# Attention and a routed mixture of experts on one core: logits of the last four tiles, stores of x, and the first passes of the second product in another order

## The chip, the cores and the metric

The kernel runs on 1 core of one Trainium2 chip. The metric is device time in microseconds (us). PE is the matrix engine, PEld its weight loads, DVE the vector engine, ACT the scalar engine, POOL the general engine (it also starts the indirect transfers), and SP the engine whose queue starts the plain transfers and the transposing ones.

## The reference

```python
def _attn_ref(q, k, v):                 # (4, 8, 768, 64)
    k_sum = k.reshape(B, H, nb, block, D).max(axis=3)      # blocks of 32
    v_sum = v.reshape(B, H, nb, block, D).mean(axis=3)
    scores_l = scale * q @ k^T, only where |i - j| < 16
    scores_s = scale * q . k_sum + log(block)
    a = softmax over [scores_l, scores_s]
    return a @ concat([v, v_sum])

def _moe_ref(x, w_gate, w_noise, noise, w1, w2):           # x is (3072, 512)
    noisy = x @ w_gate + log1p(exp(x @ w_noise)) * noise
    top2 = the two largest of 8; weights = softmax over the two
    for e in range(8):
        for k in range(2):
            mask = top2[:, k] == e
            h = maximum(x[mask] @ w1[e], 0)                # 512 -> 1024
            out[mask] += weight * (h @ w2[e])              # 1024 -> 512
```

The output of attention, heads side by side, is the x of the experts.

## The kernel before, in words

**Stages.** The 3072 tokens are 24 tiles of 128 (six for each of four batches). A loop over `t` (from -2 to 22) runs attention as a software pipeline: iteration `t` computes scores of tile `t + 2`, transposes the probabilities of tile `t + 1`, multiplies tile `t` by v (`av`, L323), and finishes tile `t - 1`: `norm` (DVE, L332 to L338) writes X in float32, `x_pe` (PE, L360) and `x_copy` (ACT, L366) make its transpose, `norm_hi` (ACT, L345, or DVE by `norm_hi_dve`, L349, for the iterations in `DVE_HI`) rounds it to float16, `norm_lo` (POOL, L352) writes what the rounding lost, and `x_out` (SP, L355) stores both halves to `xd` in DRAM. X has two buffers, the rounded pair `xr` has three, so `norm_hi` of tile t waits until the store of tile t - 3 has landed, and X of tile t until both readers of tile t - 2 are done.

**Routing.** Tiles are routed in batches of four. `gate_gt` (PE, L378) makes the logits, transposed; `gate_gc` (DVE, L385), `gate_gl` (PE, L389) and `gate_gd` (DVE, L394) turn them round; `gate_a` (ACT, L406 and L408), `gate_b`, `gate_m` (DVE, L416 to L438) pick the two best; `gate_p` (ACT, L445) makes a weight; `gate_c` (PE, L452 to L456) and `gate_d`, `gate_e` (DVE, L470 to L498) give every token its place in its expert's list; `gate_v`, `gate_o`, `gate_f` (DVE, L504 to L535) build one-hot matrices, `gate_t` (PE, L545) multiplies them, and `gate_u` (DVE, L549) adds the result to ACC, which `decode` (DVE, L556 to L562) turns into the table of token ids and weights. Batch b has tiles 4b to 4b + 3. Expert 0's first three chunks of 128 rows come only from tiles 0 to 11, so they are decoded early (`TB0`); the rest needs all six batches (`finish_table`).

**Experts.** A list holds up to 816 rows, in seven chunks. `x_gather` (POOL, L86) fetches a chunk of rows into one of four buffers `xg`, and `x_trans` (SP, L668) transposes it into `xte`. `mm1` is the first product: for each of eight slices f of the hidden width 12 matmuls (high weights by high x, low weights by high x, high weights by low x), over rows 0 to 383 (`half` 0) or 384 to 815 (`half` 1), followed by ACT's high half of h (`hth`, L691) and DVE's low half (`htl`, L692). `mm2` is the second product: for a chunk, `mm2_high` makes two passes of 8 matmuls with the high weights (by `hth`, then `htl`), `mm2_low` one with the low weights, then DVE scales (L748) and POOL scatters the result into the output. The output is first cleared by `clear` (SP, L778), eight transfers of 768 KB that read zeros from buffer 3 of `xg`.

**What sets the order.** Everything is issued in program order on each engine and each queue. In the loop, `at(time, function, ...)` puts a step behind a numbered point of an iteration (time 21.9 is near the end of iteration 21). After the loop the order is written out by hand: the end of attention, the routing of batches 3 to 5 and the first product of expert 0 (half 0) are interleaved. `og` is a PSUM tile of two banks that carries ranks (`gate_c`), table products (`gate_t`) and the product of slice 0.

Of the kernel before, what the change touches and what calls it, by code (L numbers as in the profile page):

```python
# [8 lines left out]
F32 = mybir.dt.float32  # L9
# [11 lines left out]
P = 128  # L21
# [3 lines left out]
DM = H * D  # L25
# [34 lines left out]
def attn_moe(ctx, tc, qt, kt, vt, wgn, noise, w1, w2, out):  # L60
# [289 lines left out]

    def norm_lo(t):
        nc.gpsimd.tensor_tensor(XR[t][:, DM:], X[t], XR[t][:, 0:DM], op=OP.subtract)  # L352

# [319 lines left out]

    def mm1_pe(e, half, f, ph=None):
        c0, c1 = (0, H0) if half == 0 else (H0, CAP)
        n = c1 - c0
        ph = PH[f] = bank()[:, 0] if ph is None else ph
        w = WT[e]
        x = XTE[e]
        k = 0  # L680
        for wn, xo in (("w1h", 0), ("w1l", 0), ("w1h", DC)):
            for c in range(DC):
                nc.tensor.matmul(ph[:, :n], w[wn][:, c, f * P:(f + 1) * P], x[:, xo + c, c0:c1],  # L683
                                 start=(k == 0), stop=(k == 11))
                k += 1

    def mm1_out(e, half, f):
# [45 lines left out]

    def mm2_high(e, c, hook=None):
        PY[c] = psum.tile([P, 512], F32, name="pt", bufs=2)
        mm2_pass(e, c, "w2h", HT[0], 0, PY[c])
        if hook:
            hook()
        mm2_pass(e, c, "w2h", HT[1], 1, PY[c])
# [30 lines left out]
    def at(t, f, *a):  # L770
        todo.setdefault(round(t, 3), []).append((f, a))
# [27 lines left out]
    w_alloc(0)  # L799
    W0 = [4, 6, 10, 14]  # L800
    for i in range(4):
# [7 lines left out]
    KL = [-3, -3, -3, -1, -1, -1]  # L809
    VL = [(1, 2), (7, 8), (12, 13)]  # L810
    for b in range(B - 1):
# [49 lines left out]
    for c in range(3):  # L861
        at((20.2, 20.8, 21.2)[c], x_gather, 0, c, P * BATCH[GROUP0][0])
        at((20.9, 21.2, 21.8)[c], x_trans, 0, c)

    DVE_HI = (4, 5, 8, 10, 16, 18)

# [67 lines left out]
    x_out(NT - 3)  # L934
    for i in range(4):
        clear(XG[3].bitcast(F32), 3)

# [13 lines left out]
    og = psum.tile([P, 2, 512], F32, name="o")  # L951
    gate_c(4, og)
    mm1_pe(0, 0, 0, og[:, 1])
    x_pe(NT - 2)
    x_copy(NT - 2)
    x_pe(NT - 1)
    x_copy(NT - 1)
    gate_p(4)
    for t in range(NT - 2, NT):
        norm_hi(t)  # L960
        norm_lo(t)
        x_out(t)
    for i in range(4):
        clear(XG[3].bitcast(F32), 3)
    for x in HT:
        nc.gpsimd.memset(x[:, :, CAP:], 0.0)
    gate_d(4, og)
    gate_e(4)
    gate_f(3)
    gate_gt(5)  # L970
    gate_gc(5)
    gate_gl(5)
    mm1_out(0, 0, 0)
    gate_t(3, og)
    gate_gd(5)
    gate_a(5)
    mm1_pe(0, 0, 1)
    gate_v(4)
    gate_u(3, og)
    gate_o(4)  # L980
    gate_b(5)
    gate_m(5)
    gate_p(5)
    w_hi(0, 4)
    gate_f(4)
    mm1_out(0, 0, 1)
    mm1_pe(0, 0, 2)
    gate_c(5, og)
    gate_d(5, og)
    gate_e(5)  # L990
    w_hi(0, 5)
    mm1_pe(0, 0, 3)
    gate_t(4, og)
    mm1_out(0, 0, 2)
    gate_u(4, og)
    gate_v(5)
    mm1_out(0, 0, 3)
    w_hi(0, 6)
    mm1_pe(0, 0, 4)
    gate_o(5)  # L1000
    mm1_out(0, 0, 4)
    w_hi(0, 7)
    mm1_pe(0, 0, 5)
    gate_f(5)
    mm1_out(0, 0, 5)
    for f in range(6, FC):
        mm1(0, 0, f)

    def finish_table():
        gate_t(5, og)  # L1010
        gate_u(5, og)
        decode(TB.rearrange("p e c w -> p (e c) w"), 0, NS)
# [6 lines left out]

    mm2_high(0, 0, finish_table)  # L1020
    mm2_high(0, 1)
    assert not todo, todo
    for x in PREV:
        nc.gpsimd.memset(x, 0.0)
    count_over(og)
    for c in range(2):
        mm2_low(0, c, None)
    mm2(0, 2, None)
    k = 0
# [139 lines left out]
```

## Time and profile before

| what | us |
|---|---|
| median of 3 runs | 714.16 (712.05, 714.16, 715.68) |
| profiled execution | 712.75 |
| its span, first to last instruction | 711.0 |
| PE busy, of the span | 669.7 |
| DVE / POOL / ACT busy | 318.1 / 253.3 / 233.9 |
| start of expert 0's second half of rows (first L683 with 432 columns) | 193.90 |

In the span the granted clock of PE is 0.984 of full speed in the mean. Attention fills the first 147 us, expert 0's first half of rows and the table the time to 194 us, and all the other products the rest. In rows of the timeline, the numbers are start and duration in us, and the brackets give the idle time before and what ended it.

### The profile page before, as it was taken

The page shows a single profiled execution, that of the slowest core. Times are in us where ns is not written, and L with a number is a line of the kernel's source. Part 1 is how long each engine was busy: PE and PEld are TensorE (multiplying, and loading weights), DVE is VectorE, ACT ScalarE, POOL GpSimd, SP SyncE. Part 2 cuts the span into 40 slices and gives each one's busy share as a digit, 9 for nine tenths or more (in the row PEclk, how much of TensorE's full clock was granted, in tenths as well). Part 3 has the DMA queues.
Part 4 walks back from the last instruction along what each step waited for, and adds up shares of the span by engine and source line. Part 5 has one row for each costly group of instructions (what it writes and reads, how often), then busy time and mean ns, then how long its engine had stood idle before and what let it go on. Part 6 is the DMA issues. An engine that isn't in the chain of part 4 may idle for free.

```text
span 711.0 us, 13980 instructions
## 1 busy us (share of the span) xinstructions
PE 669.7 (94%) x5552; PEld 386.2 (54%) x5552; DVE 318.1 (45%) x663; ACT 233.9 (33%) x534; POOL 253.3 (36%) x437
## 2 busy tenths in 40 slices
PE   7998879759999999999999999999999999999993
PEld 6776667536455554555455446545654555455442
DVE  5658888868542452345125413521451154222210
ACT  2978888724040450143014202410350043002100
POOL 3444445420523605632444143323424341440141
PEclk9999999989999999999999999999999999999997
DMA  9999897594682984498339525931792198210020
GB/s 288 302 253 353 260 337 240 164 341 174 164 208 64 286 218 117 145 272 256 102 82 259 182 89 132 287 125 65 177 294 82 63 212 194 90 62 27 20 86 35
DMA packets 101767, 126.26 MB, mean 178 GB/s; under 512 B 60457, under 2 KB 65329, under 8 KB 101692
## 3 DMA queue, kind: packets, MB, share of 16 engines
q1 hardware_dynamic: 89548, 89.00, 45.0%
q0 software_dynamic: 12144, 36.28, 16.7%
q8 instruction: 46, 0.75, 0.5%
q14 instruction: 29, 0.24, 0.1%
HBM read 87.57 MB, written 26.21 MB: 160 GB/s over the span
## 4 chain that ended last, share of the span: by engine, by line
PE 78%; DMA 10%; DVE 5%; ACT 2%; SPq 1%; issue 1%; POOL 1%; POOLq 0%; DVEq 0%
PE h L683 36%; PE pt L731 33%; PE pt L728 3%; DMA q<-in_qt_dram 2%; DMA stg<-in_w_dram 2%; DMA htl<-in_vt_dram 2%; DMA xg<-xd,tb 1%; DMA vw<-in_vt_dram 1%; PE s L290 1%; PE pt L310 1%; DMA xte<-xg 1%; DMA kb<-in_kt_dram 1%; DVE nm L297 1%; ACT p L304 1%; PE pt L235 1%
## 5 line engine op out<-in xcount | busy, mean ns | idle before, releaser
L683 PE MATMUL h<-xte,w1h 128*128 128x384 f16 (+1 forms) x1016 | 198.8, 337 | 0.3 <-DVE htl L692 0.2
L691 ACT ACTIVATE hth<-h 128x384 f16<-128x384 f32 (+1 forms) x127 | 64.1, 508 | 328.7 <-PE h L683 328.5
L86 POOL DMA_INDIRECT out_dram<-y,tb x48 | 56.1, 1169 | 256.2 <-DVE y L750 224.3
L683 PEld LDWEIGHTS <-w1h 128*128 128x128 f16 x1024 | 99.9, 98 | 80.1 <-issue 3.4
L731 PEld LDWEIGHTS <-hth 128*128 128x128 f16 x768 | 75.0, 98 | 91.1 <-issue 1.6
L692 DVE SCALAR_TENSOR_TENSOR htl<-h,hth 128x384 f16<-128x384 f32 (+1 forms) x127 | 73.1, 581 | 100.2 <-ACT hth L691 99.7
L683 PE MATMUL h<-xte,w1l 128*128 128x384 f16 (+1 forms) x508 | 109.0, 338 | 0.0
L750 DVE SCALAR_TENSOR_TENSOR y<-pt,tb,prev 128x512 f32<-128x512 f32 x42 | 31.5, 751 | 172.4 <-PE pt L731 168.0
L731 PE MATMUL pt<-w2l,hth 128*128 128x512 f16 x384 | 90.8, 379 | 0.5 <-DVE w2l L629 0.5
L731 PE MATMUL pt<-w2h,hth 128*128 128x512 f16 x384 | 90.7, 379 | 0.2 <-DVE y L748 0.2
L731 PE MATMUL pt<-w2h,htl 128*128 128x512 f16 x384 | 90.7, 379 | 0.0
L86 POOL DMA_INDIRECT xg<-xd,tb x56 | 61.0, 1090 | 79.8 <-DMA xte<-xg 46.6
L683 PEld LDWEIGHTS <-w1l 128*128 128x128 f16 x512 | 50.5, 99 | 39.0 <-issue 1.2
L731 PEld LDWEIGHTS <-htl 128*128 128x128 f16 x384 | 37.5, 98 | 45.1
L352 POOL TENSOR_TENSOR xr<-x,xr 128x512 f16<-128x512 f32 x24 | 28.1, 1172 | 75.7 <-ACT xr L345 50.6
L304 ACT ACTIVATE p<-s,nm 128x118 f32<-128x118 f32 x192 | 50.5, 375 | 0.8
L612 ACT ACTIVATE w2h<-stg 128x1024 f16<-128x1024 f32 x32 | 33.5, 1051 | 43.2 <-DMA stg<-in_w_dram 43.2
L629 DVE SCALAR_TENSOR_TENSOR w2l<-stg,w2h 128x1024 f16<-128x1024 f32 x32 | 38.8, 1222 | 19.6 <-ACT w2h L612 19.6
L86 POOL DMA_INDIRECT prev<-out_dram,tb x42 | 43.0, 1024 | 10.8 <-issue 10.5
L629 DVE SCALAR_TENSOR_TENSOR w1l<-stg,w1h 128x1024 f16<-128x1024 f32 x28 | 34.3, 1225 | 16.5 <-ACT w1h L612 16.5
L290 PE MATMUL s<-kx,q 64*64 64x118 f32 x768 | 26.1, 272 | 7.8 <-DMA q<-in_qt_dram 4.4
L310 PE MATMUL pt<-ident,p 128*118 128x128 f32 x192 | 29.8, 293 | 3.9 <-ACT xt L366 3.4
(162 smaller groups left out, 572.6 us busy)
## 6 DMA issues: line engine op xcount, KB each, us to landing
stg<-in_w_dram SPq DMA_DIRECT2D x64, 512.0 KB
hth<-in_vt_dram SPq DMA_DIRECT2D x8, 780.0 KB
vw<-in_vt_dram SPq DMA_DIRECT2D x32, 195.0 KB
q<-in_qt_dram SPq DMA_DIRECT2D x24, 256.0 KB
xd<-xr SPq DMA_DIRECT2D x24, 256.0 KB
out_dram<-xg SPq DMA_DIRECT2D x8, 768.0 KB
kb<-in_kt_dram SPq DMA_DIRECT2D x6, 768.0 KB
htl<-in_vt_dram SPq DMA_DIRECT2D x16, 195.0 KB
```

Source lines behind the costliest of these rows:

```text
L86: return nc.gpsimd.indirect_dma_start(**kw)
L290: nc.tensor.matmul(s[64 * blk:64 * blk + 64, a, hp, :], q[d, hp, blk], k[d, hp, blk, :], start=False, stop=hp == HP - 1, skip_group_check= ...
L304: nc.scalar.activation(PE_[t][:, a, hp, :], SC[t][:, a, hp, :], AF.Exp, bias=NM[t][:, 1, a, hp:hp + 1], scale=0.125)
L310: nc.tensor.transpose(pt[:NK, hp, :], PE_[t][:, a, hp, :], ident)
L352: nc.gpsimd.tensor_tensor(XR[t][:, DM:], X[t], XR[t][:, 0:DM], op=OP.subtract)
L612: nc.scalar.activation(WT[e][n + "h"][:, i % 4, :], SG[e, i], AF.Copy, scale=sc)
L629: nc.vector.scalar_tensor_tensor(lo, SG[e, i], sc, hi, op0=OP.mult, op1=OP.subtract)
L683: nc.tensor.matmul(ph[:, :n], w[wn][:, c, f * P:(f + 1) * P], x[:, xo + c, c0:c1], start=(k == 0), stop=(k == 11))
L691: nc.scalar.activation(hh[:, f, c0:c1], ph, AF.Relu)
L692: nc.vector.scalar_tensor_tensor(hl[:, f, c0:c1], ph, 0.0, hh[:, f, c0:c1], op0=OP.max, op1=OP.subtract)
L731: nc.tensor.matmul(py, hx[:, f, c * P:c * P + P], w[:, f, :], start=first, stop=final, skip_group_check=True)
L750: nc.vector.scalar_tensor_tensor(y, py[:, :d], gw, pv[:, :d], op0=OP.mult, op1=OP.add)
```

## The change

In the loop: the three gathers of expert 0 (`x_gather`, chunks 0 to 2) are issued together at 20.2, and their transposes move from 20.9, 21.2 and 21.8 to 21.02, 22.02 and 22.02, behind `v_load` and stores of x. The iterations 16 and 18 leave `DVE_HI`. The load of the last quarter of expert 0's w1 moves from iteration 14 to 12 (its splitting from 17.9 to 19.9 down to 15.9 to 17.9), the loads of batch 3's v from iterations 12 and 13 to 13 and 14.

Behind the loop: `norm_lo` of the last two tiles moves to DVE; the logits of batch 5 (`gate_gt`, `gate_gc`) come before the first product of slice 0, and `gate_gl` between its first four and last eight matmuls; the table steps of batches 3 and 4 come after `gate_b` and `gate_m` of batch 5; all eight clears come behind the store of tile 23; `finish_table` stands in front of the second product; there, the high passes of chunks 0, 1 and 2 come first (chunk 2 in a bank of the first product), then their low passes.

```diff
-    def norm_lo(t):
-        nc.gpsimd.tensor_tensor(XR[t][:, DM:], X[t], XR[t][:, 0:DM], op=OP.subtract)
+    def norm_lo(t, engine=nc.gpsimd):
+        engine.tensor_tensor(XR[t][:, DM:], X[t], XR[t][:, 0:DM], op=OP.subtract)
...
-    def mm1_pe(e, half, f, ph=None):
+    def mm1_pe(e, half, f, ph=None, hook=None):
...
                 k += 1
+            if hook and k == DC:
+                hook()
...
-    def mm2_high(e, c, hook=None):
-        PY[c] = psum.tile([P, 512], F32, name="pt", bufs=2)
+    def mm2_high(e, c, hook=None, py=None):
+        PY[c] = psum.tile([P, 512], F32, name="pt", bufs=2) if py is None else py
...
-    W0 = [4, 6, 10, 14]
+    W0 = [4, 6, 10, 12]
...
-    VL = [(1, 2), (7, 8), (12, 13)]
+    VL = [(1, 2), (7, 8), (13, 14)]
...
-        at((20.2, 20.8, 21.2)[c], x_gather, 0, c, P * BATCH[GROUP0][0])
-        at((20.9, 21.2, 21.8)[c], x_trans, 0, c)
-
-    DVE_HI = (4, 5, 8, 10, 16, 18)
+        at(20.2, x_gather, 0, c, P * BATCH[GROUP0][0])
+        at((21.02, 22.02, 22.02)[c], x_trans, 0, c)
+
+    DVE_HI = (4, 5, 8, 10)
...
-    for i in range(4):
-        clear(XG[3].bitcast(F32), 3)
...
-    gate_c(4, og)
-    mm1_pe(0, 0, 0, og[:, 1])
+    gate_p(4)
     x_pe(NT - 2)
     x_copy(NT - 2)
+    gate_c(4, og)
     x_pe(NT - 1)
     x_copy(NT - 1)
-    gate_p(4)
-    for t in range(NT - 2, NT):
-        norm_hi(t)
-        norm_lo(t)
-        x_out(t)
-    for i in range(4):
+    gate_d(4, og)
+    gate_e(4)
+    gate_gt(5)
+    gate_gc(5)
+    norm_hi(NT - 2)
+    norm_lo(NT - 2, nc.vector)
+    x_out(NT - 2)
+    mm1_pe(0, 0, 0, og[:, 1], lambda: gate_gl(5))
+    gate_gd(5)
+    gate_a(5)
+    norm_hi(NT - 1)
+    norm_lo(NT - 1, nc.vector)
+    x_out(NT - 1)
+    for i in range(8):
         clear(XG[3].bitcast(F32), 3)
     for x in HT:
         nc.gpsimd.memset(x[:, :, CAP:], 0.0)
-    gate_d(4, og)
-    gate_e(4)
-    gate_f(3)
-    gate_gt(5)
-    gate_gc(5)
-    gate_gl(5)
-    mm1_out(0, 0, 0)
-    gate_t(3, og)
-    gate_gd(5)
-    gate_a(5)
-    mm1_pe(0, 0, 1)
-    gate_v(4)
-    gate_u(3, og)
-    gate_o(4)
     gate_b(5)
     gate_m(5)
     gate_p(5)
+    mm1_out(0, 0, 0)
+    mm1_pe(0, 0, 1)
+    gate_c(5, og)
+    gate_f(3)
+    mm1_pe(0, 0, 2)
     w_hi(0, 4)
...
+    gate_t(3, og)
+    mm1_out(0, 0, 1)
+    gate_v(4)
+    gate_o(4)
+    mm1_pe(0, 0, 3)
+    gate_u(3, og)
+    gate_f(4)
     w_hi(0, 5)
...
+    mm1_out(0, 0, 2)
+    gate_v(5)
+    mm1_pe(0, 0, 4)
     gate_t(4, og)
+    gate_o(5)
...
     def finish_table():
-        gate_t(5, og)
-        gate_u(5, og)
...
-    mm2_high(0, 0, finish_table)
+    finish_table()
+    mm2_high(0, 0)
     mm2_high(0, 1)
+    mm2_high(0, 2, None, bank()[:, 0])
...
-    for c in range(2):
+    for c in range(3):
         mm2_low(0, c, None)
-    mm2(0, 2, None)
```

The order of instructions at three places. PE, behind the last attention output: rows of the difference from the end of `gate_c(4)` (L456) to the first matmul of slice 0 (L683); `x` is X, `xt` its copied transpose, `wg` the gate weights.

```order
 L456 LDWEIGHTS ones
 L456 MATMUL o<-m,ones 128x8
+L360 MATMUL pt<-ident,x 128x128 x4
+L378 MATMUL pt<-xt,wg_144 32x128 x16
 L683 LDWEIGHTS w1h_298
 L683 MATMUL o<-xte,w1h_298 128x384
```

The transposes of tile 23 and the logits now stand between the ranks and slice 0. The same difference behind slice 0's last matmul, where they stood:

```order
 L683 LDWEIGHTS w1h_298
 L683 MATMUL o<-xte,w1h_298 128x384
-L360 MATMUL pt<-ident,x 128x128 x8
-L378 MATMUL pt<-xt,wg_144 32x128 x16
-L389 MATMUL pt<-ident,lt 128x128
```

All of it has moved in front; L389 (`gate_gl`) is now behind slice 0's fourth matmul.

DVE, from the end of `gate_e(4)` (L498), before; `lt` and `lg` are the logits on their way round, `rh`, `lh`, `oc` the one-hot matrices, `htl` the low half of slice 0:

```order
L498 SCALAR_TENSOR_TENSOR rf<-qf,pf 128x8
L535 TENSOR_TENSOR rh<-oc,val 128x672 x2
L385 COPY lt<-pt 128x128
L692 SCALAR_TENSOR_TENSOR htl<-o,hth 128x384
L394 COPY lg<-pt 128x64
L512 TENSOR_TENSOR wa<-wa,p_2901 128x4
```

and now:

```order
L498 SCALAR_TENSOR_TENSOR rf<-qf,pf 128x8
L385 COPY lt<-pt 128x128
L352 TENSOR_TENSOR xr<-x,xr 128x512
L394 COPY lg<-pt 128x64
L352 TENSOR_TENSOR xr<-x,xr 128x512
L416 TENSOR_TENSOR nz<-sp,noi 128x32
```

The table steps and slice 0's low half went behind; the two low halves of x came in, around `lg`.

SP, from the load of w2's last quarter (L607), before; `xd<-xr` is a store of x, `xte<-xg` a transpose of gathered rows, `htl<-in_vt_dram` a v load, `out_dram<-xg_160` a clear:

```order
L607 DMA stg<-in_w_dram 128x2x512
L668 DMA_TRANSPOSE xte<-xg_157 128x8x128
L257 DMA htl<-in_vt_dram 96x520 x2
L355 DMA xd<-xr 128x1024
L668 DMA_TRANSPOSE xte<-xg_158 128x8x128
L668 DMA_TRANSPOSE xte<-xg_159 128x8x128
L355 DMA xd<-xr 128x1024 x3
L778 DMA out_dram<-xg_160 128x3x512 x4
L355 DMA xd<-xr 128x1024 x2
```

and now:

```order
L607 DMA stg<-in_w_dram 128x2x512
L257 DMA htl<-in_vt_dram 96x520 x2
L355 DMA xd<-xr 128x1024
L668 DMA_TRANSPOSE xte<-xg_157 128x8x128
L355 DMA xd<-xr 128x1024
L668 DMA_TRANSPOSE xte<-xg_158 128x8x128
L668 DMA_TRANSPOSE xte<-xg_159 128x8x128
L355 DMA xd<-xr 128x1024 x4
L780 DMA out_dram<-xg_160 128x3x512 x8
```

The last v load and the store of tile 18 passed the first transpose, the store of tile 19 the second; the clears went behind the last store (L780 is the line of `clear` in the changed kernel).

More of the change, by code (lines that the diff above doesn't have):

```diff
@@ L683, in mm1_pe @@
                 nc.tensor.matmul(ph[:, :n], w[wn][:, c, f * P:(f + 1) * P], x[:, xo + c, c0:c1],
-                                 start=(k == 0), stop=(k == 11))
+                                 start=(k == 0), stop=(k == 11), skip_group_check=hook is not None)
                 k += 1
+            if hook and k == DC:
+                hook()
     def mm1_out(e, half, f):
@@ L983, in attn_moe @@
     gate_p(5)
+    mm1_out(0, 0, 0)
[3 more added lines that the diff above has]
+    mm1_pe(0, 0, 2)
     w_hi(0, 4)
[L985 to L988, printed above, removed]
     gate_d(5, og)
     gate_e(5)
+    gate_t(3, og)
[5 more added lines that the diff above has]
+    gate_f(4)
     w_hi(0, 5)
-    mm1_pe(0, 0, 3)
+    mm1_out(0, 0, 2)
+    gate_v(5)
+    mm1_pe(0, 0, 4)
     gate_t(4, og)
-    mm1_out(0, 0, 2)
+    gate_o(5)
+    mm1_out(0, 0, 3)
     gate_u(4, og)
-    gate_v(5)
-    mm1_out(0, 0, 3)
     w_hi(0, 6)
[L999 to L1002, printed above, removed]
     mm1_pe(0, 0, 5)
     gate_f(5)
+    mm1_out(0, 0, 4)
+    mm1_pe(0, 0, 6)
     mm1_out(0, 0, 5)
-    for f in range(6, FC):
-        mm1(0, 0, f)
+    w_hi(0, 7)
+    mm1_pe(0, 0, 7)
+    gate_t(5, og)
+    mm1_out(0, 0, 6)
+    gate_u(5, og)
+    mm1_out(0, 0, 7)
     def finish_table():
-        gate_t(5, og)
-        gate_u(5, og)
         decode(TB.rearrange("p e c w -> p (e c) w"), 0, NS)
```

## The prediction, made before the result

> **What bounds the kernel now.** I read the page first, then busy time in stretches around the hand-over from attention to the experts, then the waits in 142 to 165 us, and last the engines' own timelines there. The stretches (us; busy time of PE, PEld, DVE, ACT, POOL with counts; granted clock; DMA share; GB/s):
>
> ```profile
> 146.73:149.11 2.38, 0.00 (x1) 0.03 (x2) 0.39 (x3) 0.63 (x1) 1.09 (x1) 1.00 1.09 295
> 149.11:152.52 3.41, 3.41 (x12) 1.73 (x13) 1.83 (x3) 0.00 (x0) 0.06 (x1) 0.56 0.93 353
> 152.52:159.22 6.70, 2.73 (x42) 1.95 (x40) 4.99 (x14) 2.59 (x6) 2.57 (x5) 0.97 1.05 407
> 159.22:163.20 3.98, 3.85 (x17) 2.38 (x18) 3.24 (x11) 0.46 (x2) 0.00 (x0) 0.57 1.05 406
> 163.20:176.28 13.08, 13.08 (x90) 8.14 (x89) 11.36 (x44) 6.71 (x11) 0.00 (x0) 1.00 0.36 136
> 193.90:711.00 517.10, 505.45 (x2904) 266.15 (x2903) 173.07 (x230) 114.55 (x176) 177.91 (x303) 0.99 0.54 146
> ```
>
> From 193.90, where the second half of expert 0's first product starts, PE is busy to the end; nothing the change touches lies there, so those 517.1 us stay and only the start of that half can move. The loss is between 146.73 and 163.20: PE idles for 2.38 us, runs 3.41 us at a clock of 0.56, is busy for 2.73 of 6.70 us, and then runs at 0.57 again. What ends those waits (waiter, releaser, total us, times, longest):
>
> ```profile
> PE pt L389 <- DVE lt L385: 3.6, 1, 3.6
> PE o L683 <- DMA xte<-xg: 2.4, 1, 2.4
> DVE pos L470 <- PE o L683: 1.7, 1, 1.7
> ACT xr L345 <- DMA xd<-xr: 3.8, 1, 3.8
> ```
>
> So PE first waits for transposed rows; then it computes product 0, while DVE's ranks of tiles 16 to 19 wait for that product in the same tile; then DVE is late with the copy of the last logits. ACT's 3.8 us goes on to POOL and from POOL to DVE, as the next rows show: the x of tile 23 starts at 149.20, after 2.05 us of waiting.
>
> **The table's chain, step by step.** After the change DVE runs nearly without a break, so I lay its steps out from 145.65, where it starts to normalise tile 22. All times in this part are on the clock of the trace before. Prices are distances between starts in these rows (start, busy us, engine, line, operation):
>
> ```profile
> 143.69 0.18 DVE L416 TENSOR_TENSOR nz<-sp,noi 128x32 f32<-128x32 f32 x1
> 145.65 0.16 DVE L332 TENSOR_SCALAR r<-s 128x8 f32<-128x8 f32 x1
> 146.76 0.15 DVE L332 TENSOR_SCALAR r<-s 128x8 f32<-128x8 f32 x1
> 149.20 0.69 DVE L338 TENSOR_TENSOR x<-s,ri 128x512 f32<-128x512 f32 x1 [2.05 <-POOL xr L352]
> 155.14 2.26 POOL L352 TENSOR_TENSOR xr<-x,xr 128x512 f16<-128x512 f32 x2 [5.97 <-ACT xr L345]
> 156.35 1.07 DVE L498 SCALAR_TENSOR_TENSOR rf<-qf,pf 128x8 f16<-128x8 f16 x1
> 166.91 0.18 DVE L470 TENSOR_TENSOR pos<-o,bs 128x32 f32<-128x32 f32 x1
> 168.33 0.55 DVE L692 SCALAR_TENSOR_TENSOR htl<-h,hth 128x384 f16<-128x384 f32 x1
> 169.03 0.16 DVE L512 TENSOR_TENSOR wa<-wa,p 128x4 f32<-128x4 f32 x1
> 170.12 0.55 DVE L692 SCALAR_TENSOR_TENSOR htl<-h,hth 128x384 f16<-128x384 f32 x1
> 170.59 0.68 DVE L504 TENSOR_TENSOR lh<-iotar,rf 128x512 f16<-128x512 f16 x1
> 171.72 0.55 DVE L692 SCALAR_TENSOR_TENSOR htl<-h,hth 128x384 f16<-128x384 f32 x1
> 172.19 1.62 DVE L535 TENSOR_TENSOR rh<-oc,val 128x672 f16<-128x672 f16 x2
> 173.72 0.55 DVE L692 SCALAR_TENSOR_TENSOR htl<-h,hth 128x384 f16<-128x384 f32 x1
> 178.79 0.33 DVE L549 TENSOR_TENSOR acc<-acc,o 128x168 f32<-128x168 f32 x1 [1.23 <-PE o L545]
> 180.47 1.02 POOL L86 DMA_INDIRECT xg<-xd,tb  x1 [22.76 <-DVE oc L561]
> ```
>
> That gives: one norm 1.11 (145.65 to 146.76); gate_b with gate_m 1.96 (143.69 to 145.65); gate_d with gate_e 1.42 (166.91 to 168.33); gate_v 1.09; one low half of h 0.47 (170.12 to 170.59); gate_o 1.13; gate_f 1.53; gate_u 0.3; from the last gate_u to the first gather of the remaining rows 1.68 (178.79 to 180.47). PE's, ACT's and the clears' prices:
>
> ```profile
> 137.64 1.08 PE L378 MATMUL pt<-xt,wg 128*32 128x128 f32 x32 [0.35 <-ACT pts L313]
> 167.90 0.74 PE L545 MATMUL o<-rh,lh 128*128 128x168 f16 x8
> 171.08 0.81 PE L683 MATMUL h<-xte,w1l 128*128 128x384 f16 x4
> 173.03 0.81 PE L683 MATMUL h<-xte,w1l 128*128 128x384 f16 x4
> 188.45 1.89 PE L731 MATMUL pt<-w2h,hth 128*128 128x512 f16 x8 [0.20 <-DVE y L748]
> 190.17 1.89 PE L731 MATMUL pt<-w2h,htl 128*128 128x512 f16 x8
> 193.90 0.89 PE L683 MATMUL h<-xte,w1h 128*128 128x432 f16 x4
> 154.43 1.15 ACT L345 ACTIVATE xr<-x 128x512 f16<-128x512 f32 x2
> 159.90 0.23 ACT L406 ACTIVATE e<-lg 128x32 f32<-128x32 f32 x1 [3.94 <-DVE wa L512]
> 160.16 0.23 ACT L408 ACTIVATE sp<-e 128x32 f32<-128x32 f32 x1
> out_dram<-xg SPq DMA_DIRECT2D x8, 768.0 KB
> ```
>
> One product of 12 matmuls takes 1.95 (171.08 to 173.03), a pass of 8 in the second product 1.72, gate_t about 0.6.
>
> *Transposed rows.* PE now asks for them only after the logits, at about 150.3. The three gathers stand one behind another on POOL, right after the table of the first ids, and no cast or low half of POOL stands between them. The last transpose landed at 149.1 before (146.73 plus 2.38), with one store of x less in front of it, but with the second and third gather behind a low half on POOL. Even without any gain there the wait of 2.4 is covered by the logits; if it came back, each us later than 150.3 would cost one.
>
> *Stores of x.* The store of tile 18 goes ahead of the first transpose, so ACT's cast of tile 21 and POOL's low half no longer wait. X of tile 23 then needs no buffer that is held: two norms end at 145.65 + 2.22 = 147.87. Next late is DVE itself.
>
> *Logits first.* gate_o(3) to 149.0, gate_d(4) and gate_e(4) to 150.4: they no longer wait 1.7 for product 0, and no POOL work runs beside them, which in the rows at 155.14 and 156.35 goes with an operation on 8 elements taking 1.07. On PE the transposes of tile 23 start at 147.9; with their four matmuls (0.6), ACT's copy (0.65) and gate_gt (1.08) the logits are there at 150.3. The copy lt ends at 150.6, norm_lo of tile 22 on DVE at 151.3. That operation is new on DVE: I take 0.69, the row of x at 149.20, of the same size; POOL's 1.13 (half of 2.26) is the upper bound, and the low half of h, of the same kind on three quarters of the size, at 0.55 the lower one. PE runs four matmuls of product 0 (0.65) and turns the logits round by 151.25, and lg is copied by 151.45.
>
> *A new wait.* The diff puts norm_lo(23) on DVE behind norm_hi(23), which stands on ACT behind gate_a(5). From lg that is 0.49 (159.90 to the end of sp), 0.58 for the cast and some 0.15 of hops, so DVE idles to 152.7. Behind it queue gate_b(5) and all later steps: norm_lo to 153.4, gate_b and gate_m to 155.3, product 0's low half (ACT's part ends at 155.6) to 156.1, gate_f(3) 157.6, gate_d and gate_e(5) 159.05, low half 1 159.5, gate_v(4) 160.6, gate_o(4) 161.75, gate_u 162.05, gate_f(4) 163.55.
>
> *PE behind it.* Product 0 ends at 152.55, product 1 at 154.5; gate_c(5) waits for gate_m to 155.4; product 2 ends at 157.45, gate_t(3) at 158.2, products 3 and 4 at 162.1. There PE waits 1.5 for gate_f(4), and gate_t(4) ends at 164.2. Products 5 to 7 (5.85) end at 170.05, and gate_t(5) at 170.6; DVE's last gate_f is done at 163.55 + 0.47 + 2.22 + 0.47 + 0.3 + 1.53 = 168.55, in time.
>
> *Table and second product.* The last gate_u starts at 170.75, and one low half (0.47) now stands between it and the decoding, so the gathers start at 170.75 + 0.47 + 1.68 = 172.9 against 180.47. From there to the second half's first matmul before took 193.90 - 180.47 = 13.43 (four gathers, four transposes), which gives 186.3. PE's own way is 9 passes of 1.72 = 15.5 from 170.6, to 186.1: high passes of three chunks first leave DVE 10.3 us for the low weights, so that wait is gone, but the end is set by the rows. The half starts at 186.3 instead of 193.90: 7.6 us gained.
>
> *Attention's last tiles.* Two casts go from DVE to ACT, and the last quarter of expert 0's first weights is loaded and split two tiles earlier, the last v loads one tile later.
>
> ```profile
> 108.47 0.43 DVE L349 CAST xr<-x 128x512 f16<-128x512 f32 x1 [0.92 <-DMA xd<-xr]
> L622 DVE SCALAR_TENSOR_TENSOR w1l<-stg,w1h 128x512 f16<-128x512 f32 x3 | 2.1, 685 | 0.0
> 105.28 1.04 PE L290 MATMUL s<-kx,q 64*64 64x118 f32 x32 [1.75 <-DMA q<-in_qt_dram]
> ```
>
> For DVE this is at most 2 x 0.43 + 0.92 + 2 x 0.69 = 3.2 less; on the other side ACT gets two casts of 0.58, and 512 KB instead of the 390 of half a batch of v go ahead of a q for which PE waits already: 122 KB at 353 to 407 GB/s are 0.3. Between +3.2 and -1.5 I take +0.5, nearer to the lower end, because what DVE is rid of, ACT takes on.
>
> **Sum.** 7.6 + 0.5 = 8.1 us. The profiled run took 712.75 us, of which the span is 711.0; less 8.1 that is 704.65. Its time is 1.41 below the median of the three runs (714.16; 712.05 to 715.68). From the median the sum would be 706.06; I forecast between the two, 705.3.
>
> **The rivals.** *The clock drops again.* The clock was 0.56 for 3.41 us after an idle stretch of 2.38, and after the change PE still waits for DVE's x of tile 22 (its norm ends at 146.76 in the steps above) and in two shorter gaps behind it. Against it stands that none of these is as long as 2.38. If it drops, gate_gt and the first four matmuls of product 0 take about 0.45 + 0.65 longer, and DVE's chain waits for both: 7.0 gained, 706.4. The Trainium skill, page "TensorE: Matmul & The Clock Gate", Part 1, says that the clock falls to half after an idle window of about 3.4 us and comes back after as long of work. By that rule alone no gap of the changed kernel is long enough and the sum would stay at 705.3. The trace agrees on the way back (3.41 us) but not on the fall, which came after 2.38 us of idling.
>
> *A late v load.* Half of batch 3's v is now asked for one tile later, behind a q in a queue on which PE already waits for q. Its sums stand on PE in front of tile 16's output. If it lands 2 to 4 us late, PE and then ACT lose that: 709.0 at 3.7. For it: the wait of 1.75; against it: it is asked for two and a half tiles ahead of its use.
>
> *Slower: the clears hold the gathers.* All eight clears of the output now queue on SP behind the store of tile 23, at about 153.8 instead of 149.6, and the first gather of the remaining rows writes the tile that they read, so POOL waits for all of them. 8 x 768 KB = 6.29 MB at 407 GB/s are 15.5 us, to 169.3: 3.6 us of cover. The case decides from 6.29 MB in 19.1 us, 329 GB/s, downwards; at 295 GB/s, as in the first stretch, 2.2 are lost; with 36 us or more, under 175 GB/s, the gathers start after 189.8, 9.3 later than before, and the kernel takes 713.4 (between profiled run and median, as above) + 9.3 - 0.5, about 722.
>
> **How the numbers follow.** About 0.5%, 3.6 us, is what a measurement of this kernel can tell from no change. Chances: forecast 0.60; clock 0.18; late v load 0.13, of which a quarter is too late for a gain that shows; clears or something else late in the table's chain 0.09, half of it so far that nothing is left and half of it slower. Faster: 0.60 + 0.18 + 0.10 = 0.88; same 0.03 + 0.05 = 0.08; slower 0.04. The range: below, the attention term at its upper end (2.7 more) and 1.0 for the spread of the runs, 701.6; above, the late v load and half a us for norm_lo at POOL's price, 709.5.
>
> **What would show it.** Right: no wait of PE for xte before product 0, logits (L378) within 5 us of the last attention output, a DVE wait of about 1.1 ahead of the second norm_lo, a PE wait of about 1.5 at the second gate_t, no DVE operation of 1 us on 8 elements there, the second half of the first product starting 7 to 9 us sooner. Wrong: a clock under 0.9 in two stretches again, the first of the four gathers waiting for the clears, or the same start of that half. If PE waits for L235 in tile 16, the v load was late.

## The result, and the profile after

The changed kernel takes 711.09 us in the median of 20 runs (705.99 to 716.01), against 714.99 of before measured beside it in 20 runs: ratio 0.9937, 95% interval 0.9913 to 0.9962. Two further sets of the same two kernels give 0.9921 (0.9887 to 0.9955) and 0.9932 (0.9894 to 0.9969). It is faster, by 4.5 us (2.7 to 6.2) by the first ratio and by 3.9 by the medians. The forecast of 705.3 is 5.8 too low, and the time lies 1.6 above the upper end of the range. The profiled execution took 709.13, its span is 707.3 at a granted clock of 0.984.

The stretches of the changed kernel around the hand-over (columns as in the prediction's table):

```profile
145.00:150.00 5.00, 2.58 (x68) 2.27 (x68) 4.66 (x25) 1.56 (x4) 1.48 (x4) 1.00 0.37 121
150.00:155.00 5.00, 4.34 (x56) 3.09 (x57) 4.38 (x17) 2.00 (x5) 0.00 (x0) 1.00 0.00 0
155.00:160.00 5.00, 3.56 (x27) 2.10 (x26) 4.12 (x22) 2.90 (x7) 0.00 (x0) 1.00 0.70 267
160.00:165.00 5.00, 5.00 (x37) 3.25 (x36) 4.83 (x20) 2.31 (x4) 0.00 (x0) 1.00 1.05 401
165.00:170.00 5.00, 4.68 (x34) 2.90 (x33) 4.93 (x12) 1.88 (x4) 0.00 (x0) 1.00 1.05 408
170.00:175.00 5.00, 5.00 (x34) 3.00 (x33) 4.26 (x12) 1.28 (x3) 0.00 (x0) 1.00 0.76 292
```

The clock is 1.00 throughout, DVE is busy nearly all the time, and the DMA engines, full from 149 to 163 before, are empty from 150 to 155, busy behind that, and full from 160 to beyond 170. PE's waits from 132 to 192 us (waiter, releaser, total, times, longest):

```profile
PE pt L378 <- ACT pts L313: 2.5, 1, 2.5
PE pt L360 <- DVE r L332: 2.5, 1, 2.5
PE h L683 <- DMA xte<-xg: 1.5, 1, 1.5
PE o L452 <- DVE htl L694: 1.4, 1, 1.4
```

The wait of 3.6 for the copy of the last logits and the one for transposed rows in front of slice 0 are gone. The second, for the norm of tile 22 (at 150.04), stands where PE waited for rows before. New are also the first (logits of batch 4, at 139.21), the third (in front of the second half of rows) and the fourth. The milestones of the prediction, in the timelines of PE, DVE and POOL:

```profile
95.65 1.04 PE L290 MATMUL s<-kx,q 64*64 64x118 f32 x32
148.70 0.16 DVE L332 TENSOR_SCALAR r<-s 128x8 f32<-128x8 f32 x1
155.72 0.69 DVE L352 TENSOR_TENSOR xr<-x,xr 128x512 f16<-128x512 f32 x1 [1.14 <-ACT xr L345]
173.35 0.33 DVE L549 TENSOR_TENSOR acc<-acc,o 128x168 f32<-128x168 f32 x1 [0.64 <-PE o L545]
175.13 0.22 DVE L561 TENSOR_TENSOR oc<-acc 128x56 f32<-128x56 f32 x1
176.71 1.54 POOL L86 DMA_INDIRECT xg<-xd,tb  x1 [28.44 <-DVE tl L645]
190.41 0.89 PE L683 MATMUL h<-xte,w1h 128*128 128x432 f16 x4 [1.54 <-DMA xte<-xg]
```

These are the scores of tile 16, the norm of tile 22, its new wait on DVE (1.14; 1.1 was predicted), the last `gate_u`, the end of the table, the first gather of the remaining rows, and the second half. The half starts at 190.41 instead of 193.90; behind it 516.9 us follow, 517.1 before. So the whole difference of the two profiles lies ahead of it, as supposed, but is 3.49 and not 8.1. Of what is missing, 2.76 lie ahead of the scores of tile 16 (95.65 against 92.89), where the 14 profiles of this case scatter from 92.51 to 98.41, with no order early or late throughout. The gather stands 1.58 behind the start of L561; before it stood 0.23 behind (180.24 to 180.47). The chain of waits says what it stood for:

```profile
165.99 9.70 DMA out_dram<-xg
175.68 0.02 issue
175.71 0.04 POOLq L86
...
176.01 0.52 issue
...
176.71 1.54 POOL xg L86
```

The last clear, issued at 165.99, landed at 175.68, and 1.03 us later POOL had gone through its waits and began. That is the rival "the clears hold the gathers". The experiments had to show what it costs, and what the rest of the shortfall is.

To compare executions I use three legs between milestones: from the scores of tile 16 to the norm of tile 22, from there to the last `gate_u`, from there to the second half.

### The profile page after: what moved, and what is told of

Read it like the earlier page. It is cut to its first block, busy times and chain, and to the rows that moved or that the text cites. A ratio compares the mean times of both kernels' runs of the same rounds, so it can differ in the third digit from the quotient of the medians.

```text
span 707.3 us, 13983 instructions
## 1 busy us (share of the span) xinstructions
PE 668.8 (95%) x5552; PEld 386.4 (55%) x5552; DVE 314.6 (44%) x663; ACT 235.5 (33%) x536; POOL 250.8 (35%) x435
## 4 chain that ended last, share of the span: by engine, by line
PE 75%; DMA 8%; DVE 7%; ACT 4%; SPq 2%; issue 2%; POOL 1%; another core or an unknown queue 0%; POOLq 0%; DVEq 0%; ACTq 0%
PE h L683 33%; PE pt L733 33%; PE pt L730 3%; DMA vw<-in_vt_dram 2%; DMA q<-in_qt_dram 2%; ACT p L304 1%; DMA out_dram<-xg 1%; SPq L780 1%; PE s L290 1%; PE pt L310 1%; DVE nm L297 1%; PE pt L235 1%; PE o L323 1%; DMA kb<-in_kt_dram 1%; DVE x L338 1%
## 5 line engine op out<-in xcount | busy, mean ns | idle before, releaser
L683 PE MATMUL h<-xte,w1h 128*128 128x384 f16 (+1 forms) x1016 | 198.3, 336 | 1.6 <-DMA xte<-xg 1.5
L683 PEld LDWEIGHTS <-w1h 128*128 128x128 f16 x1024 | 99.4, 98 | 78.4 <-issue 3.7
L683 PE MATMUL h<-xte,w1l 128*128 128x384 f16 (+1 forms) x508 | 108.4, 336 | 0.0
L733 PE MATMUL pt<-w2h,htl 128*128 128x512 f16 x376 | 88.8, 379 | 0.0
L733 PE MATMUL pt<-w2h,hth 128*128 128x512 f16 x376 | 88.8, 379 | 0.0
L733 PE MATMUL pt<-w2l,hth 128*128 128x512 f16 x376 | 88.7, 379 | 0.0
L683 PEld LDWEIGHTS <-w1l 128*128 128x128 f16 x512 | 50.1, 98 | 38.1
L352 POOL TENSOR_TENSOR xr<-x,xr 128x512 f16<-128x512 f32 x22 | 25.5, 1159 | 68.1 <-ACT xr L345 55.6
```

What stands on the lines that cost most here:

```text
L352: engine.tensor_tensor(XR[t][:, DM:], X[t], XR[t][:, 0:DM], op=OP.subtract)
L733: nc.tensor.matmul(py, hx[:, f, c * P:c * P + P], w[:, f, :], start=first, stop=final, skip_group_check=True)
```

## The experiments

### The change once more

Nothing edited, twice (e1_same and g4_same):

> The changed kernel once more, nothing edited. In its first profile the second half of expert 0's first product started at 190.41 us (193.90 before), and two things in front of it were late against the prediction: the scores of tile 11 started 2.8 us later than before (112.62 + 7.1 against 117.32 for tile 12, say), and ACT (L313) and DVE idled 2.1 and 1.3 us at 136.5 to 138.5 for no releaser that the profile names. Theory 1 (the late start of the norms is scatter of this execution, not part of the change): ACT's stall at 136 to 139 is not there or under 0.5 us, the norm of tile 22 starts at 146 or earlier instead of 148.70, the second half at 187.5 to 188.5, and the time is about 709. Theory 2 (the stall belongs to the change: the three gathers now stand one behind another on POOL while stores and loads fill the queues): the stall is there again, over 1.5 us, at the same place, the norm of tile 22 starts at 148 to 149, the second half within 0.7 us of 190.4, and the time is about 711.

> The changed kernel a third time, as the neighbour of g2_buffer_again and g3_clears_early on the same chip. Theory: 709 to 711.5, the first gather of the remaining rows 1.5 to 1.6 us behind L561, a PE wait of 1.7 to 2.5 us in front of L378 at 135 to 140 us, PE waiting 1.5 to 3.1 us for xte in front of the second half. Rival (the two earlier profiles were alike by chance): one of these three is gone.

709.58 us (ratio 0.9921) and 711.87 (0.9932); spans of the profiles 705.4 and 711.5. The norm of tile 22 starts at 144.29 and 146.40 against 148.70 in the first profile, so its late start was scatter, as theory 1 said. The scatter is not in one place: the scores of tile 16 start at 92.51 and 95.64 against 95.65, so 3.1 of the first repeat's 4.4 us lie ahead of them, and all of the second repeat's 2.3 behind them. But the wait ahead of L378 is there each time, with 1.94 and 0.96 (the second under the 1.7 that I expected at least), so theory 2 is right that a stall comes with the change. And the second half is late each time (PE waits 3.1 and 2.9 for rows); of the first repeat:

```profile
171.61 0.22 DVE L561 TENSOR_TENSOR oc<-acc 128x56 f32<-128x56 f32 x1
173.20 1.53 POOL L86 DMA_INDIRECT xg<-xd,tb  x1 [29.34 <-DVE tl L645]
188.46 0.89 PE L683 MATMUL h<-xte,w1h 128*128 128x432 f16 x4 [3.10 <-DMA xte<-xg]
```

1.59 again from L561 to the gather, and a longer wait for rows. What the first profile did not have is a slow clock behind PE's wait for the norm of tile 22. PE's timeline in the first repeat, and the stretches around that wait:

```profile
145.63 0.80 PE L360 MATMUL pt<-ident,x 128*128 128x128 f32 x4 [2.45 <-DVE r L332]
```

```profile
143.00:145.60 2.60, 0.18 (x7) 0.04 (x2) 2.36 (x12) 0.20 (x1) 0.86 (x4) 1.00 0.88 254
145.60:149.60 4.00, 3.76 (x44) 2.79 (x45) 3.33 (x14) 1.71 (x3) 0.00 (x0) 0.57 0.00 0
149.60:155.00 5.40, 4.45 (x35) 2.57 (x27) 3.73 (x23) 1.71 (x6) 0.00 (x0) 1.00 0.36 136
```

The leg from the norm to the last `gate_u` takes 24.65 in the first profile, 25.54 and 26.70 in the repeats (clock 0.50 from 148.3 to 155.1 in the last, from 146.0 to 149.3 in the first repeat): the rival "the clock drops again" occurs in two executions of three. The same wait of 2.45 or 2.46 stands in five more of the profiles below (e2_other_buffer, g2_buffer_again, g3_clears_early, e3_gathers_apart, f4_cast_first), and the clock falls to 0.50 behind each of them: seven of eight.

### Other buffers for the last gathers

```diff
         last_ids()
+        gi[0] = 4
         for c in range(3, NCH):
```

The four gathers then write buffers 0, 1, 2, 3, and only the last of them the one that the clears read. On the changed kernel, twice (e2_other_buffer, g2_buffer_again), and on the kernel before as a control (f2_before_buffer):

> The changed kernel, but the four gathers of expert 0's remaining rows take the buffers 0, 1, 2, 3 in place of 3, 0, 1, 2, so that only the last of them writes the buffer that the clears of the output read. Theory (the clears hold the gathers): in the changed kernel the gather stood 3.36 us behind the table product's sum (acc, L549) where before it stood 1.68 to 2.15 behind it; now it stands 2.2 or less behind it, the second half of the first product starts about 1.2 us sooner relative to the last L549, and the time is about 1.2 us under that of the changed kernel beside it. The fourth gather then comes 3 to 4 us later and finds the clears done. Rival (the gather waited for the table's decoding and for DVE's and POOL's own steps): the distance stays at 3.0 to 3.4 us and the time stays within 0.4 us of the changed kernel.

> e2_other_buffer once more, beside the changed kernel on the same chip, because 6 runs gave 705.76 with an interval of 0.8% that still touches that of the changed kernel. Theory (the clears hold the gathers): 2.5 to 4 us under the changed kernel beside it; the first gather of the remaining rows 0.2 to 0.3 us behind L561. Rival (e2_other_buffer had lucky runs): within 1 us of the changed kernel.

> The kernel before with the one edit of e2_other_buffer: the four gathers of the remaining rows take the buffers 0, 1, 2, 3. In the kernel before the first of these gathers followed DVE's L561 by 0.23 us, the clears being long done, so nothing should hold it. Theory (the edit pays only because the change put all clears behind the last store): no gain, within 1 us of the kernel before (714.9), the gather again 0.2 to 0.3 us behind L561. Rival (another rotation of the buffers is better by itself, for the later experts too): 2 to 4 us are gained here as well, and then e2_other_buffer shows nothing about the clears.

On the changed kernel 705.76 us (704.68 to 708.33; ratio to before 0.9863, 0.9821 to 0.9904) and 707.93 (0.9894, 0.9853 to 0.9935). The first of the two:

```profile
171.85 0.22 DVE L561 TENSOR_TENSOR oc<-acc 128x56 f32<-128x56 f32 x1
172.09 1.02 POOL L86 DMA_INDIRECT xg<-xd,tb  x1 [28.57 <-DVE oc L561]
177.53 0.93 POOL L86 DMA_INDIRECT xg<-xd,tb  x1 [0.23 <-issue]
185.43 0.89 PE L683 MATMUL h<-xte,w1h 128*128 128x432 f16 x4
```

The gather follows L561 by 0.24, the fourth gather no longer finds a clear in its way, and PE reaches the second half without any wait: 15.37 us behind the last `gate_u`, 15.36 in the repeat, where the changed kernel took 17.06, 18.63 and 18.45. So the hold costs 1.7 to 3.3 us, more than the 1.35 of the gather alone and the 1.2 expected: behind a held gather the rows were late as well. The control took 714.13 against 713.93 (ratio 1.0001, 0.9977 to 1.0024), its gather 0.23 behind L561, as in the kernel before. The other rotation by itself is worth nothing that shows (the interval reaches 1.7 us to either side).

### Four clears earlier

```diff
     x_out(NT - 3)
+    for i in range(4):
+        clear(XG[3].bitcast(F32), 3)
...
-    for i in range(8):
+    for i in range(4):
         clear(XG[3].bitcast(F32), 3)
```

> The changed kernel with four of the eight clears back behind the store of tile 21 as before, the other four behind the store of tile 23, and the buffers as in the changed kernel. Theory (it is the time at which the clears end that holds the gathers): with 3.1 MB less behind the last store, the clears end about 7 us sooner, the first gather follows L561 by 0.2 to 0.3 us instead of 1.58, and the time is that of e2_other_buffer, 705 to 707.5. Rival (any 8 clears in front of the gather cost it 1.35 us, because POOL looks at 8 queue semaphores one after another): the gather stays 1.4 to 1.6 us behind L561 and the time is that of the changed kernel. Third case: the clears now stand in front of the stores of tiles 22 and 23 and delay what waits for them; then ACT waits for a buffer of xr again.

707.25 us (704.64 to 711.38), ratio 0.9897 (0.9855 to 0.9939). The buffers are those of the changed kernel, and eight clears still stand ahead of the gather, yet:

```profile
177.34 0.22 DVE L561 TENSOR_TENSOR oc<-acc 128x56 f32<-128x56 f32 x1
177.58 1.02 POOL L86 DMA_INDIRECT xg<-xd,tb  x1 [28.27 <-DVE oc L561]
190.92 0.89 PE L683 MATMUL h<-xte,w1h 128*128 128x432 f16 x4
```

0.24 again, no wait for rows, 15.36 from the last `gate_u`. It is the time at which the clears end that holds the gather, not their number and not the buffers. Two different edits remove the wait and give the same leg; that the clears hold the gathers is shown.

### The two halves of the change by themselves

The changed kernel with the loop of before (e4_tail_only):

```diff
-    W0 = [4, 6, 10, 12]
+    W0 = [4, 6, 10, 14]
...
-    VL = [(1, 2), (7, 8), (13, 14)]
+    VL = [(1, 2), (7, 8), (12, 13)]
...
-        at(20.2, x_gather, 0, c, P * BATCH[GROUP0][0])
-        at((21.02, 22.02, 22.02)[c], x_trans, 0, c)
+        at((20.2, 20.8, 21.2)[c], x_gather, 0, c, P * BATCH[GROUP0][0])
+        at((20.9, 21.2, 21.8)[c], x_trans, 0, c)
...
-    DVE_HI = (4, 5, 8, 10)
+    DVE_HI = (4, 5, 8, 10, 16, 18)
```

and the kernel before with the same lines the other way round (f3_loop_only):

> The changed kernel with the loop as it was before: gathers at 20.2, 20.8, 21.2, their transposes at 20.9, 21.2, 21.8, the loads of the last quarter of w1 in iteration 14 and of v in 12 and 13, and six iterations whose cast DVE does. What stands behind the loop is the changed one. If the steps behind the loop (logits ahead of slice 0, the order of the table steps, high passes first) carry the gain, the time is 711 to 712.5, and PE waits about 2 us for transposed rows at no place, since the logits cover it. If the transposes ahead of the stores in SP's queue are what held ACT's cast of tile 21 (5.97 us of POOL's waiting before), the x of tile 23 is late again by about 2 us and the time is 712 to 714. If the loop's edits cost (the stall at 136 to 139 us), the time is under that of the changed kernel by up to 2 us.

> The kernel before with the changes inside the loop alone: three gathers together at 20.2, transposes at 21.02 and 22.02 behind the stores, the last quarter of w1 in iteration 12, v in 13 and 14, two casts back on ACT; what stands behind the loop is that of before. The other half alone, e4_tail_only, took 714.86 against 714.85 of before. Theory (the halves need each other): the transposed rows of slice 0 now come behind two stores while slice 0 still stands first, so PE's wait for xte before slice 0 stays at 2 us or grows; x of tile 23 no longer waits 2.05; together 0 to 2 us gained, 713 to 715. Rival (the loop's edits carry the gain and the order behind the loop is worth nothing): 709.5 to 711.5.

The order behind the loop alone takes 714.86 against 714.85 (ratio 0.9983, 0.9949 to 1.0018), the loop alone 710.55 against 713.93 (0.9942, 0.9916 to 0.9968). For the first I had expected 711 to 714, and none of its cases came true in the time; for the second 713 to 715, and there the rival did (709.5 to 711.5): the loop by itself pays as much as the whole change. PE's waits in it, from 135 to 200 us, hold none for `xte` in front of slice 0, though its transposes stand behind two stores:

```profile
PE pt L389 <- DVE lt L385: 3.7, 1, 3.7
PE pt L378 <- issue: 2.5, 1, 2.5
PE o L452 <- DVE m L438: 1.0, 1, 1.0
```

In it ACT no longer waits for a store, and the norm of tile 23 follows that of tile 22 by 1.11; with the order behind the loop alone ACT waits 2.21 for a store again and DVE 1.05 for its x. Of the loop's changes only the place of the gathers was tried by itself (below), so which of the others pays stays open.

The legs of all five orders (us; before has two profiles, the second from the control, whose order differs in the buffers alone; the loop alone and the order behind it have one each):

| leg | predicted | before | loop alone | behind the loop alone | changed kernel | clears not in the way |
|---|---|---|---|---|---|---|
| scores 16 to norm 22 | 52.26 | 52.76, 52.09 | 52.87 | 52.52 | 53.05, 51.78, 50.76 | 51.35, 51.40, 51.33 |
| norm 22 to last `gate_u` | 25.10 | 33.14, 30.56 | 27.80 | 27.63 | 24.65, 25.54, 26.70 | 26.11, 26.72, 25.82 |
| last `gate_u` to second half | 15.55 | 15.11, 14.81 | 14.82 | 18.47 | 17.06, 18.63, 18.45 | 15.37, 15.36, 15.36 |
| together | 92.9 | 101.0, 97.5 | 95.5 | 98.6 | 94.8, 96.0, 95.9 | 92.8, 93.5, 92.5 |

Behind the loop, the new order takes some 2.2 us out of the second leg (27.80 to a mean of 25.63) and puts 3.2 into the third (14.82 to a mean of 18.05): its gain is given back to the clears.

### The gathers apart

```diff
-        at(20.2, x_gather, 0, c, P * BATCH[GROUP0][0])
+        at((20.2, 20.8, 21.2)[c], x_gather, 0, c, P * BATCH[GROUP0][0])
```

> The changed kernel, but the three gathers of expert 0's first rows are issued at 20.2, 20.8 and 21.2 as before, the second and third behind a low half of x on POOL; their transposes stay where the change put them. Theory 2 of the run beside it (the gathers one behind another cause ACT's and DVE's stall at 136 to 139 us): no idle stretch of ACT over 1 us there, the norm of tile 22 starts 1.5 to 3 us sooner against the scores of tile 23 than in the changed kernel (148.70 - 134.42 = 14.3), and the time is 1.5 to 2.5 us less. Theory 1 (scatter): both kernels show the same distance, and the same time within 0.7 us. Third case: the transposed rows come later because the gathers wait behind the low halves on POOL; then PE waits for xte in front of slice 0 (none in the changed kernel) and up to 2 us are lost.

709.89 us (ratio 0.9917, 0.9887 to 0.9948), as the changed kernel. The wait ahead of L378 is gone (0.35), and the norm of tile 22 comes 12.3 behind the scores of tile 23, against 14.3, 13.0 and 12.0 in the changed kernel; the first two would give a gain, the third none. The time shows none, so theory 2's price falls, though not its stall. The gathers are held here too (1.58; the third leg is 19.29).

### The wait for the cast, the clock, and everything together

In front of `gate_b(5)` DVE idles 1.14 for a cast on ACT, and PE idles 2.45 for the norm of tile 22. On top of the other buffers, the cast goes first (f4_cast_first); then PE's gap is filled as well (f5_warm); then the gathers are apart as well (g1_together):

```diff
-    gate_a(5)
     norm_hi(NT - 1)
+    gate_a(5)
     norm_lo(NT - 1, nc.vector)
```

```diff
     og = psum.tile([P, 2, 512], F32, name="o")
+    for i in range(24):
+        nc.tensor.matmul(og[:, i % 2, 0:P], identb, identb, start=True, stop=True, skip_group_check=True)
```

> e2_other_buffer with one swap on ACT: the cast of tile 23 (norm_hi) ahead of gate_a(5) in place of behind it. In the changed kernel DVE idled 1.14 us for that cast in front of the second norm_lo, as predicted. Theory: the idle time falls to under 0.2 us, DVE's chain, PE's ranks c5 and the last L549 come about 1.0 us sooner against the norm of tile 22, and the time is 0.7 to 1.1 under that of e2_other_buffer (705.8), about 704.8. Rival: the next wait takes it all (the logits are late by the cast's 0.6, since ACT then does e and sp later, and DVE waits for sp in front of gate_b); then the wait for sp appears at L416 with 0.6 to 1.1 us and the time is that of e2_other_buffer within 0.4.

> f4_cast_first with 24 matmuls of 128 columns (some 1.95 us by L226, 90 in 7.30 us) on PE in the gap of 2.45 us in which it waits for the norm of tile 22; they write og, and the ranks written there later do not read them. The granted clock fell to 0.5 for about 3.3 us behind that gap in the profiles of e1_same (from 146.0), e2_other_buffer (from 147.9) and e4_tail_only (from 151.9), though not in the first profile of the changed kernel. Theory (the idle stretch costs the clock, and the slow logits and slice 0 delay the table's chain): the clock is 1.00 from 143 to 155 us, the norm of tile 22 to the last L549 takes 24.7 less 1.0 in place of 26.1 less 1.0, and the time is 0.8 to 1.5 less than f4_cast_first. Rival 1: the clock falls all the same (the fill is too short). Rival 2: it stays up and DVE or the rows set the end anyway, time within 0.4.

> f5_warm with the three gathers of expert 0's first rows apart again (20.2, 20.8, 21.2), so it has four edits on the changed kernel: other buffers for the last gathers, the cast of tile 23 ahead of gate_a(5), the 24 filling matmuls, the gathers apart. In all six profiles with the three gathers one behind another PE waited 1.75 to 2.53 us in front of the logits of batch 4 (L378, at 135 to 140 us), in all four with them apart 0.35 us. Theory: that wait is 0.35 here, nothing else is late, and 1 to 2 us come off f5_warm (707.5 with a spread of 705.8 to 711.2): about 705 to 706, the best of all. Rival (the stall is only moved: DVE's chain of tile steps sets the norm of tile 22, and the second and third gather now collide with POOL's low half and DVE later): the norm of tile 22 comes as late as with the gathers together (12.5 to 14 us behind the scores of tile 23, 12.2 in e3_gathers_apart) and the time is that of f5_warm within 0.7.

706.10 (0.9894, 0.9859 to 0.9929), 707.53 (0.9907, 0.9872 to 0.9943) and 706.31 (0.9885, 0.9846 to 0.9925). Inside the leg from the norm to the last `gate_u` each edit does what it should: 24.70 with the cast first (the mean with other buffers alone is 26.41), and 23.53 and 23.52 with PE filled. Expected were 704.8 us, then 0.8 to 1.5 less than that run, then 705 to 706. With the cast first `norm_lo` and `gate_b` follow without a wait:

```profile
154.18 0.69 DVE L352 TENSOR_TENSOR xr<-x,xr 128x512 f16<-128x512 f32 x1
154.81 0.19 DVE L416 TENSOR_TENSOR nz<-sp,noi 128x32 f32<-128x32 f32 x1
```

and with PE filled its wait is 1.01, and the clock stays up (in both kernels) where it fell in the repeat above:

```profile
148.50:151.00 2.50, 1.52 (x28) 1.34 (x24) 2.26 (x9) 0.20 (x1) 0.76 (x4) 1.00 0.54 200
151.00:156.00 5.00, 4.34 (x56) 3.08 (x57) 4.79 (x18) 2.52 (x6) 0.00 (x0) 1.00 0.02 3
```

But none of the three is measurably under the kernel with other buffers alone (0.9863 and 0.9894). The second leg has 1.7 and 2.9 us, the times do not show them, with 6 runs each and a spread of 704 to 711. In the first of the three the profile gives them back: its first leg is 54.17, with 2.46 in front of L378, and the three legs take 94.2 together, against 92.9 with the clears out of the way alone. In the other two they take 91.3 and 90.1, and there it stays open; stretches that no edit of these three touches differ more than that, 92.51 to 98.41 ahead of the scores of tile 16 and 516.8 to 520.0 behind the second half, over all profiles. All six sets of runs (five kernels) in which the clears are out of the way have medians from 705.76 to 707.93, the changed kernel in three sets 709.58 to 711.87. The simplest of the five, one line on top of the change, is as good as any: its medians are 3.8 and 3.9 us under those of the changed kernel beside it (709.58 and 711.87), and 9.1 and 7.3 under before (714.85 and 715.18).

## Why the prediction missed, step by step

**The region and the mechanism were right.** What follows the second half is unchanged but for scatter (516.9 to 520.0 in the changed kernel, 517.1 and 517.9 before), the logits come first, PE does not wait for rows in front of slice 0, x of tile 23 no longer waits for a store, DVE waits 1.14 for its cast (1.1), and from the norm of tile 22 to the last `gate_u` the first profile took 24.65 (25.1). Of PE's waits the one at `gate_c(5)` was 1.4, for slice 0's low half in the same tile, not for `gate_m` (0.9), and the one at the second `gate_t` 0.3 (1.5).

**The failed step is the cover of the clears.** "8 x 768 KB = 6.29 MB at 407 GB/s are 15.5 us, to 169.3: 3.6 us of cover." The clears were issued from 8.10 us behind the norm of tile 22 (8.15 predicted), but landed 18.9 us after the first issue (156.80 to 175.68), and POOL needed 1.03 more. The rate was right; what the sum left out is in the same stretch us by us (the last two lines are fifths of a us):

```profile
172.00:173.00 1.00, 1.00 (x11) 0.74 (x10) 0.71 (x2) 0.23 (x1) 0.00 (x0) 1.00 1.05 401
173.00:174.00 1.00, 1.00 (x9) 0.54 (x7) 0.65 (x2) 0.26 (x1) 0.00 (x0) 1.00 0.55 209
174.00:175.00 1.00, 1.00 (x6) 0.49 (x5) 0.90 (x6) 0.00 (x0) 0.00 (x0) 1.00 0.10 37
175.00:176.00 1.00, 1.00 (x7) 0.44 (x5) 0.85 (x6) 0.00 (x0) 0.00 (x0) 1.00 0.02 8
175.20:175.40 0.20, 0.20 (x3) 0.09 (x1) 0.17 (x2) 0.00 (x0) 0.00 (x0) 1.00 0.03 10
175.40:175.60 0.20, 0.20 (x3) 0.08 (x2) 0.18 (x1) 0.00 (x0) 0.00 (x0) 1.00 0.00 0
```

The first bytes move 0.4 us behind the first issue, and the store of tile 23 (0.26 MB, some 0.6 us) moves in the same stretch: the plain queue moved 6.55 MB from 156 to 176. Nearly all of it has moved by about 173.4, and the last landing comes 2.3 us later. The Trainium skill, page "DMA: Bandwidth & Descriptors", section "Anatomy of one DMA — SWDGE (gpsimd) path", gives about 2.0 us of fixed cost to a transfer, most of it until the last byte is confirmed in the target memory. The trace has an end of that size, from SP's queue, but it is not that: bytes trickle at 72 down to 10 GB/s until 175.4, with 0.19 down to 0.03 of the DMA engines busy, and the landing follows the last of them by 0.3 to 0.5 us (0.2 to 0.6 in the repeats). I priced the clears by bandwidth alone. I had the rival, with the point from which it decides (19.1 us), and gave it 0.09; 18.9 + 1.03 is just beyond that point. Its price was read wrongly too: of the 1.7 to 3.3 only 1.35 is the gather's own delay; the rest is rows that land 13.70 to 15.26 us behind the first gather instead of the 13.43 I took. Why they land later then is not settled.

**The second failed step is the yardstick.** All prices were differences to one execution of before. It has 101.0 us over the three legs; a second one, of an order that takes the same time, 97.5. The 2.4 for rows ahead of slice 0 is 1.3 there, and the second leg 30.56 instead of 33.14. Against the mean, 99.2, about 1.75 us of the forecast gain was never there to be had, as far as two executions say.

**The terms add up.** 8.1, less 1.75 for the yardstick, less 2.6 for the hold (95.5 as the mean of the changed kernel, 92.9 with the clears out of the way), leaves 3.75; the legs themselves give 99.2 - 95.5 = 3.7, and the times 4.5 (2.7 to 6.2). With the clears out of the way the legs take 92.9 in the mean, which is the predicted figure, but in part by luck: the first leg is 51.4 instead of 52.26, and the second 26.2 instead of 25.10, with a slow clock in all three profiles. The time itself missed by 5.8, of which 1.6 are the point that the forecast counted from: 713.4, between one run and a median of three, where the median of 20 is 714.99.

**Attention's last tiles** were given 0.5; the first leg went from a mean of 52.4 to one of 51.9. No late v load appeared: PE's only wait for L235 there is 0.7, and for ACT.

**The clock.** "None of these is as long as 2.38" was wrong: PE waits 2.45 for the norm of tile 22, and the clock fell behind it in two profiles of three, and in seven of the eight in which that wait stands, where the prediction gave it 0.18; the second leg is 0.9 and 2.05 us longer there (25.54 and 26.70 against 24.65; 1.1 was the rival's price). By the rule of the Trainium skill, page "TensorE: Matmul & The Clock Gate", Part 1, quoted in the prediction, no gap was long enough; the trace does not agree. That page also calls the window free-running, and the trace fits that: the same gap was followed by a fall in seven executions, at once in some and 2.5 us after PE had resumed in one (e2_other_buffer, 145.29 to 147.8), and by none in one; the slow stretch lasted about 3.4 us in five of them and about 6.8 in two. Why a gap of 2.45 suffices is not shown; filled down to 1.01, it was followed by no fall in two executions.

## What to carry to other kernels

A transfer that is "covered" has to be timed from its first issue to its last landing, and up to the waiting engine's next instruction, not by bytes over rate: here that was 19.9 us instead of 15.5, and a cover of 3.6 us was none. When an order moves transfers behind the last store, look which buffer they read and who writes it next; one line that gives the next writer another buffer brought almost as much as the whole change. And take a second profile of before, or its repeat in a control, ahead of summing up waits: two executions of one order (but for the buffers of four gathers) differed by 3.5 us here.

## What the runs showed of the hardware

Three indirect gathers issued one behind another go with a stall of the engines that work beside them. In all nine profiles with the gathers together PE stands 0.96 to 2.53 us in front of L378, in the five with them apart 0.35 or 0.36. With them together (the changed kernel's first profile) and apart (the last experiment):

```profile
139.21 1.08 PE L378 MATMUL pt<-xt,wg 128*32 128x128 f32 x16 [2.53 <-ACT pts L313]
```

```profile
137.21 1.08 PE L378 MATMUL pt<-xt,wg 128*32 128x128 f32 x32 [0.36 <-ACT pts L313]
```

In six of the nine the wait is shown as "issue", that is, for nothing that the profile names. What it is for was not found, and no difference in time that shows goes with it here.
